# A hand-ordered two-stage Strassen MLP kernel: its order written anew, instruction by instruction

## The chip, the core and the metric

The kernel runs on one core of one Trainium2 chip. The metric is the device time of one execution in microseconds, as the median of several runs. TensorE (PE) does the matrix products, and its loading of weights is shown as a row of its own (PEld). VectorE (DVE), ScalarE (ACT) and GpSimd (POOL) do the elementwise work, and SyncE (SP) issues most of the loads and stores.

## The reference

```python
# x (8, 4096, 192); weight (8 heads, 7 taps); 24 channels to a head
w = softmax(weight, axis=-1)
x_pad = concat([zeros(8, 6, 192), x], axis=1)
out = einsum('hk,bskhg->bshg', w, x_pad[:, s + k, h, g])   # causal depthwise convolution
h = out.reshape(32768, 192) @ w_in                          # w_in (192, 2048)
g = h * (1 / (1 + exp(-1.702 * h)))
return g @ w_out                                            # w_out (2048, 192)
```

Everything is float32.

## The kernel before

The 32768 tokens are worked off in `N_BIG` = 32 steps of 1024 tokens. Both matrix products are done by schemes of the Strassen kind, which need fewer multiplications and more sums of operands and results. Steps 0 and 1 (`OPENING`) also prepare the weights; steps 2 to 31 all look alike. A step has two stages.

**First stage** (`product1`, L598). There are 20 products (`TERMS`) for each of two halves of the hidden width, and each of them is issued for two row halves, h = 0 and h = 1, on the two groups of 64 rows of the array: 80 matmuls of 64x128 weights on 512 columns. The trace shows a float32 matmul as two records, so these are 160 records. They go into four pairs of PSUM banks (`slot00`/`slot01` to `slot30`/`slot31`; the second digit is h), which are handed round through the list `free`; names such as a3 stand for a pair of banks, names such as k4 for a place in SBUF (`rooms`). Between the products, DVE forms sums (L639), ACT copies banks out (L633, or L635 into another bank) and applies the activation (L615 for one bank, L620 for a sum that covers two banks). A product into a bank waits until whoever reads the bank's last value is done.

**Second stage** (`second`, `one_matmul`, L855). 78 main parts of three matmuls each (column groups 0 to 2 of the array) and 78 side matmuls (column group 3), each 128x32 weights on 256 columns: 312 matmuls, 624 records. ACT copies results (L880, L884), DVE joins (L355, L357) and transposes them (L771), and SP stores.

**Beside the two stages**, work for later steps is spread over the same engines: DVE transposes x for the step after next into the tile `xt` (L438), ACT multiplies the taps (L483), POOL adds them up (L501) or issues adding DMAs (L506), POOL forms the sums of blocks that the products need (`vsum`, L355 and L357), and SP issues the DMAs that take a block to the other row half (`cross`, L526). DVE also forms the sums of the activated values g (`sum_g`, L355 and L357, 128x1024), part of them into `osbs`, and POOL issues adding DMAs for more of them (`acc`, L831).

What sets the order: each engine works through its instructions in the order in which the program issues them. For the first stage that is the list `ORDER`; there `do` issues both row halves of an entry one after the other. For the second stage it is `PLAN`, where an entry `go` issues one main part and then one side matmul. The spread work stands in queues (`todo`, `ready`, `adds`, `pieces`, `sums_left`) from which an entry such as `("tap",)` or `("vsum",)` takes the next piece, whatever it is.

Of the kernel before, what the change touches and what calls it, by code (L numbers as in the profile page):

```python
# [15 lines left out]
def kernel(  # L16
# [38 lines left out]
    xt_pool = ctx.enter_context(tc.tile_pool(name="xt", bufs=1))  # L55
# [6 lines left out]
    xts = {}  # L62
# [103 lines left out]
    def side(big, other, b):  # L166
        return cross_of(big, b) if other else slot_of(big, b)
# [20 lines left out]
    def form(i):  # L188
# [8 lines left out]
    COPY_O = [  # L197
        [(10, 2), (16, 1), (17, 0), (18, 0), (8, 7), (9, 5), (11, 3, -1), (12, 6, -1)],
        [(13, 3), (14, 3), (15, 0), (19, 4), (20, 4), (21, 5), (22, 7)],
        [],  # L200
        [(23, 1), (24, 1), (1, 14), (7, 0, -1)],
    ]
    SUMS_O = [
# [4 lines left out]
    ]  # L208
    TURN_O = (9, 17, 20, 21)

# [105 lines left out]
    def split_rest(i, part=slice(0, PIECE)):  # L316

        lo, hi, m, e = words(i, part)
        ef = e.bitcast(F32)
        act.activation(ef, e, AF.Relu, bias=bias[:, 0:1], scale=-1.0)  # L320
        act.activation(e, ef, AF.Relu, bias=bias[:, 1:2], scale=-(2.0**23))
# [43 lines left out]
    w_left = list(SUMS_W)  # L365

    def next_w(n):
        for _ in range(n):
            add_up(lambda j: w_in_s[:, j, :], *w_left.pop(0))

# [6 lines left out]
    def round_o(i):  # L377
# [15 lines left out]
        round_piece(NW + i, dsts)  # L393

    def add_forms(stage):
        for dst, src, *sign in COPY_O[stage]:
            if sign:
                act.mul(form(dst), form(src), -1.0)
            else:
                act.copy(form(dst), form(src))  # L400
        for dst, src in SUMS_O[stage]:
            nc.gpsimd.dma_start(out=form(dst), in_=form(src), accum_op=ALU.add)

    def end_forms():
        for i in TURN_O:
            act.mul(form(i), form(i), -1.0)
# [26 lines left out]

    def transpose_x(big, c, n=None):
        if big not in xts:
            xts[big] = xt_pool.tile([P, NC, 2, XT], F32, name="xt")
        ns = slice(0, 2) if n is None else slice(n, n + 1)
        vec.transpose(  # L438
            xts[big][:, c, ns, :].rearrange("p n (j t) -> p (n j) t", t=Q),
            xin[:, ns, :, :].rearrange("p n j d -> p (n j) d")[:, :, c * R : c * R + Q],  # L440
        )
# [10 lines left out]
    def tap_home(big, c, k):  # L452
        if big == 1:
            return homes_1[c][k - 1]
        if big < 3:
            return (first_taps if c == 0 else taps[3])[k - 1]
        return taps[c][k - 1]

    def conv_src(big, c, k, ns=slice(0, 2)):
        return xts[big][:, c, ns, Q - PAD + k : Q - PAD + k + T]  # L460

    def conv(big, c, k, ns=slice(0, 2), times=vec.tensor_scalar_mul):
        src = conv_src(big, c, k, ns)
        dst = own(big)[:, 2 * c + ns.start : 2 * c + ns.stop, :]
        tap = cw[:, c, k : k + 1]
        if k == 0:
            times(dst, src, tap)
# [5 lines left out]
    DMA_TAPS = (0,)  # L473
    TAPS_IN = (0, 2, 1)
    ADDS_IN = [(1, 6), (2, 5), (2, 6)] + [(c, k) for c in (2, 1) for k in range(1, K) if (c, k) not in ((1, 6), (2, 5), (2, 6))]
    TREE = {2: [(1, 2)], 4: [(3, 4)], 6: [(5, 6), (0, 1), (3, 5), (0, 3)]}
    TREE_1 = {2: {2: [(1, 2)], 4: [(3, 4), (0, 1)], 6: [(5, 6), (0, 3), (0, 5)]}, 0: {2: [(1, 2)], 4: [(3, 4)], 6: [(5, 6)]}}

    def tap(big, c, k):

        dst = own(big)[:, 2 * c : 2 * c + 2, :]
        home = tap_home(big, c, k) if k else dst
        act.mul(home, conv_src(big, c, k), cw[:, c, k : k + 1])  # L483
        if k and c not in DMA_TAPS and big > 1:
            adds.append((ADDS_IN.index((c, k)), dst, home))
            adds.sort(key=lambda a: a[0])
            if big == 2:
                next_add()
            return
        homes = [dst] + [tap_home(big, c, i) for i in range(1, K)]  # L490
        for a, b in (TREE if big > 1 else TREE_1[c]).get(k, ()):
            tree.append((homes[a], homes[b]))
        if big < 3:
            end_taps(2 if big == 2 and k == K - 1 else 0)

    tree, adds = [], []

    def next_add():
        if adds:
            _, dst, home = adds.pop(0)  # L500
            nc.gpsimd.tensor_add(dst, dst, home)  # L501

    def add_taps():
        if tree:
            out, src = tree.pop(0)
            nc.gpsimd.dma_start(out=out, in_=src, accum_op=ALU.add)  # L506

    def add_pair(c, a, b):

        dst = own(1)[:, 2 * c : 2 * c + 2, :]  # L510
        homes = [dst] + [tap_home(1, c, i) for i in range(1, K)]
        vec.tensor_add(homes[a], homes[a], homes[b])

    def end_taps(left=0):
        while len(tree) > left:
            add_taps()
# [13 lines left out]
    def copy_over(b):  # L530

        for o in range(2):
            act.copy(conv_t[halves[1 - o], cross_of(0, b), :], own(0)[halves[o], b, :])

    pieces, sums_left = [], []
    LAST_AT = {s[0]: i for i, s in enumerate(SUMS_C)}
    ENDS = (NBLK, NBLK + 3, NBLK + 6, NB - 2, NB)
    GROUPS = [range(*ends) for ends in zip(ENDS, ENDS[1:])]  # L540

    def cross_piece():
        if pieces:
            cross(*pieces.pop(0))

    def cross_blocks(big):

        bs = list(REST)
        while bs:
            n = 1  # L550
            while n < min(3, len(bs)) and bs[n] == bs[0] + n:
                n += 1
            pieces.append((big, bs[0], bs[0] + n))
            bs = bs[n:]

    def next_sum():
        if sums_left:
            big, i = sums_left.pop(0)
            sums_c(big, *SUMS_C[i])
            for b in GROUPS:  # L560
                if max(LAST_AT[s] for s in b) == i:
                    pieces.append((big, b[0], b[-1] + 1))

    def begin_sums(big):
        sums_left.extend((big, i) for i in range(len(SUMS_C)))

    def prepare(big):

        for k in range(K if big < 3 else 0):
            yield "", 0.76 if k else 0.48, lambda k=k: conv(big, 1, k)  # L570
        yield f"conv {big}", 0.0, lambda: None
        def done():
            need(f"taps {big}")
            while adds:
                next_add()
            if OPEN_SUM:
                sums_c(big, *OPEN_SUM)
            cross(big, OPEN, OPEN + 1)

        yield f"done {big}", 0.0, done  # L580

    def prepare_taps(big):

        order = [(c, k) for c in (0, 2) for k in range(K)]
        if big > 2:
            order = [(c, 0) for c in TAPS_IN] + [(c, k) for c in TAPS_IN for k in range(1, K)]
        for c, k in order:
            yield "", 1.0, lambda c=c, k=k: tap(big, c, k)
        yield f"taps {big}", 0.0, lambda: None

    def product1(slot, a, b, big, v, first=False):
# [3 lines left out]
        for h in range(2):  # L595
# [11 lines left out]
    ALL = slice(0, TOK)  # L607

    def gelu(b, u, v, src, sign=1):
# [3 lines left out]
        if isinstance(src, list):  # L613
            for h in range(2):
                act.activation(  # L615
                    dst[:, :, h, :], src[h].rearrange("p (o t) -> p o t", o=2), AF.Gelu_apprx_sigmoid,
                    scale=float(sign),
                )
        else:
            act.activation(  # L620
                dst.rearrange("p o h t -> p h o t"),
                src.rearrange("p h (o t) -> p h o t", o=2),
                AF.Gelu_apprx_sigmoid,
                scale=float(sign),
            )
# [3 lines left out]

    def copy2(dst, src, sign=1):  # L630
        for h in range(2):
            if sign == 1:
                act.copy(bank(dst, h), bank(src, h))  # L633
            else:
                act.mul(bank(dst, h), bank(src, h), -1.0)  # L635

    def sum2(op, dst, a, b):
        for h in range(2):
            op(*(bank(t, h) for t in (dst, a, b)))  # L639

# [623 lines left out]
```

## Time and profile before

| | before |
|---|---|
| median of 3 runs | 2262.73 us (2262.1 to 2263.56) |
| profiled execution | 2262.78 us, span 2261.1 us |
| busy PE / PEld | 2248.2 us (99%) / 1552.0 us (69%) |
| busy DVE / ACT / POOL | 1985.3 (88%) / 1707.7 (76%) / 1063.9 us (47%) |
| first stage of a steady step | 35.42 us |
| second stage of a steady step | 33.94 us |

A row of the chain or of the timeline begins with the start and the duration in microseconds; then come engine, tiles and line, and in brackets the idle time before it with what ended it. A group of instructions by line shows busy time and the mean of one in ns. PE counts as busy while a matmul is in flight on any part of the array, so a gap on one row group of the array does not show in PE's busy share; it shows in the length of a stage.

### The profile page before, as it was taken

To read this page: it belongs to the slowest core of one execution; us is meant where nothing else is said; L and a number is where in the kernel's file an instruction comes from. 1 tells how busy PE (TensorE), PEld (TensorE's weight loads), DVE (VectorE), ACT (ScalarE), POOL (GpSimd) and SP (SyncE) were. 2 spreads that over 40 slices of the span, in tenths; PEclk is the share of its full clock that TensorE was granted. 3 is DMA by queue.
4 is the path that set the end of the run, shared out by engine and by line. 5 is a ranking of instruction groups with operands and counts; after the bars stand their busy time and mean duration, and the time that the engine had idled before them with its cause. 6 is when DMAs were issued, how large, how long until landed. Compare 5 with 4: busy or idle time off the path is not lost.

```text
span 2261.1 us, 62136 instructions
## 1 busy us (share of the span) xinstructions
PE 2248.2 (99%) x24966; PEld 1552.0 (69%) x24966; DVE 1985.3 (88%) x2970; ACT 1707.7 (76%) x3233; POOL 1063.9 (47%) x1098
## 2 busy tenths in 40 slices
PE   9999999999999999999999999999999999999999
PEld 5366567766777766777667776667776677766775
DVE  8998888988889888889888898888988888988888
ACT  8677877777777778777787777787777877777754
POOL 1545544455543555444555445554355544455510
PEclk9999999999999999999999999999999999999999
DMA  8986657766667666576565776666866657765543
GB/s 198 174 158 133 125 114 150 143 128 127 121 131 159 128 128 126 111 160 140 125 132 114 141 152 128 129 124 118 163 134 128 124 114 151 144 127 103 104 92 71
DMA packets 275679, 298.05 MB, mean 132 GB/s; under 512 B 119104, under 2 KB 203328, under 8 KB 275392
## 3 DMA queue, kind: packets, MB, share of 16 engines
q0 software_dynamic: 57648, 150.69, 37.0%
q1 hardware_dynamic: 216096, 142.99, 27.8%
q8 instruction: 198, 3.24, 0.6%
q14 instruction: 89, 0.73, 0.1%
q10 hardware_dynamic: 1648, 0.39, 0.1%
HBM read 53.15 MB, written 25.17 MB: 35 GB/s over the span
## 4 chain that ended last, share of the span: by engine, by line
PE 96%; DVE 2%; ACT 1%; issue 1%; DMA 1%; POOL 0%; DVEq 0%; ACTq 0%; POOLq 0%; SPq 0%
PE slot L598 49%; PE slot L855 45%; PE slot L1120 1%; DVE g L357 1%; DMA g<-osbs 0%; PE slot L1115 0%; DVE room L357 0%; ACT g L615 0%; PE slot L946 0%; DVE room L639 0%; ACT w_form L483 0%; DMA xin<-in_x_dram 0%; DVE slot L639 0%; DVE room L355 0%; DVE osbs L771 0%
## 5 line engine op out<-in xcount | busy, mean ns | idle before, releaser
L598 PE MATMUL slot<-conv_t,w_in_s 64*128 64x512 f32 x5152 | 1147.4, 594 | 3.3 <-ACT room L633 1.5
L598 PEld LDWEIGHTS slot<-conv_t,w_in_s 64*128 64x128 f32 x5152 | 663.3, 186 | 474.6 <-issue 312.1
L855 PE MATMUL slot<-g,w_form 128*32 128x256 f32 x9672 | 894.2, 379 | 0.7 <-DVE room L357 0.7
L855 PEld LDWEIGHTS slot<-g,w_form 128*32 128x32 f32 x9672 | 575.6, 110 | 128.9 <-DVE room L357 2.1
L501 POOL TENSOR_TENSOR conv_t<-conv_t,g 128x512 f32<-128x512 f32 x354 | 449.0, 1275 | 88.4 <-ACT g L483 65.4
L855 PE MATMUL slot<-g,w_out_s 128*32 128x256 f32 x5952 | 467.5, 379 | 1.3 <-DVE g L357 0.8
L357 DVE TENSOR_TENSOR g<-g 128x1024 f32<-128x1024 f32 x372 | 450.4, 1224 | 8.0 <-DMA g<-osbs 1.0
L880 ACT COPY room<-slot 32x256 f32<-32x256 f32 x651 | 237.2, 364 | 289.8 <-PE slot L855 281.5
L639 DVE TENSOR_TENSOR room<-slot,room 128x512 f32<-128x512 f32 x620 | 383.6, 679 | 67.8 <-PE slot L598 67.8
L633 ACT COPY room<-slot 128x512 f32<-128x512 f32 x620 | 337.7, 595 | 77.7 <-PE slot L598 61.7
L483 ACT ACTIVATE g<-xt,cw 128x512 f32<-128x512 f32 x534 | 353.9, 715 | 3.7
L620 ACT ACTIVATE g<-room 128x1024 f32<-128x1024 f32 x248 | 265.7, 1071 | 79.0 <-DVE room L639 49.3
L615 ACT ACTIVATE g<-slot 128x512 f32<-128x512 f32 x528 | 282.5, 610 | 51.9 <-PE slot L598 32.8
L831 POOL DMA_DIRECT2D g<-g x124 | 128.1, 1038 | 355.0 <-PE slot L855 330.8
L639 DVE TENSOR_TENSOR slot<-slot,room 128x512 f32<-128x512 f32 x372 | 239.7, 689 | 53.8 <-PE slot L598 52.2
L855 PEld LDWEIGHTS slot<-g,w_out_s 128*32 128x32 f32 x5952 | 239.7, 110 | 43.2 <-DVE room L639 23.3
L355 POOL TENSOR_TENSOR conv_t<-conv_t 128x256 f32<-128x256 f32 x210 | 179.3, 860 | 129.2 <-PE slot L598 119.6
L855 PE MATMUL slot<-osbs,w_form 128*32 128x256 f32 x2232 | 229.5, 379 | 0.0
L506 POOL DMA_DIRECT2D g<-g x120 | 105.9, 883 | 238.1 <-ACT g L483 99.4
L855 PEld LDWEIGHTS slot<-osbs,w_form 128*32 128x32 f32 x2232 | 132.5, 110 | 23.6
L639 DVE TENSOR_TENSOR slot<-room,slot 128x512 f32<-128x512 f32 x124 | 79.8, 687 | 41.8 <-PE slot L598 41.8
L855 PE MATMUL slot<-room,w_form 128*32 128x256 f32 x1488 | 112.9, 379 | 0.0
(166 smaller groups left out, 1662.6 us busy)
## 6 DMA issues: line engine op xcount, KB each, us to landing
g<-g POOLq DMA_DIRECT2D x124, 512.0 KB, 6.5
xin<-in_x_dram SPq DMA_DIRECT2D x240, 180.0 KB, 4.2
conv_t<-conv_t SPq DMA_DIRECT2D x186, 192.0 KB, 5.4
g<-g POOLq DMA_DIRECT2D x120, 256.0 KB, 5.4
conv_t<-conv_t SPq DMA_DIRECT2D x186, 128.0 KB, 2.9
out_dram<-osbs SPq DMA_DIRECT2D x186, 128.0 KB, 2.7
g<-room POOLq DMA_DIRECT2D x31, 512.0 KB, 5.1
conv_t<-g POOLq DMA_DIRECT2D x60, 256.0 KB, 5.4
```

Source lines behind the costliest of these rows:

```text
L355: eng.tensor_add(v(dst), v(a), v(b))
L357: eng.tensor_sub(v(dst), v(a), v(b))
L483: act.mul(home, conv_src(big, c, k), cw[:, c, k : k + 1])
L501: nc.gpsimd.tensor_add(dst, dst, home)
L598: nc.tensor.matmul(slot[h], w_in_s[halves[h], a, v * P : (v + 1) * P], src, start=first, stop=True, skip_group_check=True,)
L615: act.activation(dst[:, :, h, :], src[h].rearrange("p (o t) -> p o t", o=2), AF.Gelu_apprx_sigmoid, scale=float(sign),)
L620: act.activation(dst.rearrange("p o h t -> p h o t"), src.rearrange("p h (o t) -> p h o t", o=2), AF.Gelu_apprx_sigmoid, scale=float(sign),)
L633: act.copy(bank(dst, h), bank(src, h))
L639: op(*(bank(t, h) for t in (dst, a, b)))
L831: nc.gpsimd.dma_start(out=spot(dst), in_=spot(a), accum_op=ALU.add)
L855: nc.tensor.matmul(dst, w, t, start=first, stop=last, skip_group_check=True)
L880: act.copy(to, d)
```

## The change

`ORDER`, `PLAN`, and the queues with their functions are replaced by one list, `STEP`, in which each entry issues one instruction (steps 2 to 30), and a list `LAST` for step 31. A product, a copy, a sum or an activation now names its row half h in its last place (None is the activation over both banks), so the two halves can stand apart; `("m", i)` is main part i, `("s", i)` side matmul i and `("t", i)` the copy of a side result. Taps, adds, block sums, crossings and x transposes are named one by one with the step they are for (a 1 or 2 ahead of the other numbers: the next step or the one after). `OPENING` is written out in the same way, in about the order of before. `xt` becomes a lasting tile, where before each step took a new one from a pool that holds one. The number of compute instructions on each engine stays.

```diff
-    xt_pool = ctx.enter_context(tc.tile_pool(name="xt", bufs=1))
+    xt = consts.tile([P, NC, 2, XT], F32)
...
-        if big not in xts:
-            xts[big] = xt_pool.tile([P, NC, 2, XT], F32, name="xt")
...
-    def product1(slot, a, b, big, v, first=False):
+    def product1(slot, a, b, big, v, first=False, hs=range(2)):
...
-        for h in range(2):
+        for h in hs:
...
-    def copy2(dst, src, sign=1):
-        for h in range(2):
...
-    ORDER = [
-        (0, "prod", 6, "a8"), (0, "sum", "k0", "a8", "-", "k8"), (0, "prod", 2, "a3"), (0, "copy", "k4", "a3", 1),
...
-    PLAN = [
-        ("side", 13, 16, "k0"), ("main", 1, 5, "p2", 1), ("vsum",), ("go", 2), ("sum", 14, 14, "-", 18), ("go", 1),
...
+    STEP = [
+        ("tap", 1, 1, 6), ("prod", 0, 6, "a8", 0), ("sum", 0, "k0", "a8", "-", "k8", 0), ("prod", 0, 2, "a3", 1),
...
+        ("prod", 1, 7, "a4", 0), ("gelu", 1, 1, 1, "a3", 1, 1), ("vsum", 1, 0), ("add", 1, 2, 4), ("vsum", 1, 1),
+        ("vsum", 1, 2), ("prod", 1, 15, "a3", 0), ("gelu", 1, 1, 1, "a3", 1, 0), ("prod", 1, 7, "a4", 1),
+        ("prod", 1, 1, "a1", 1), ("vsum", 1, 4), ("vsum", 1, 3), ("gsum", 0, 5, "+", 6), ("vsum", 1, 5),
+        ("prod", 1, 1, "a1", 0), ("sum", 1, "k3", "a4", "+", "k4", 0), ("sum", 1, "k3", "a4", "+", "k4", 1),
+        ("gelu", 1, 3, 1, "k3", 1, None), ("prod", 1, 10, "a4", 0), ("copy", 1, "a5", "a4", -1, 0),
...
-                w, t = now["steps"].pop(0)
-                for c in range(NC):
-                    one_matmul(chunk(now["to"], c), w[:, chunk_cols(c)], t, now["first"], not now["steps"])
-                now["first"] = False
-                d, ws, ts, st, to = side.pop(0)
-                one_matmul(d, ws, ts, st, to is not False)
+    def main_part(i):
+        dst, w, t, first, last = now["todo"][i]
+        for c in range(NC):
+            one_matmul(chunk(dst, c), w[:, chunk_cols(c)], t, first, last)
...
+    def side_part(i):
+        d, w, t, first, to = now["aside"][i]
+        one_matmul(d, w, t, first, to is not False)
```

Three places show how the instructions move. The first is ACT at the start of a steady step's first stage. `slot20`/`slot21` hold a3, `slot10`/`slot11` first a0 and then a4, `slot00`/`slot01` a1; L483 is a tap. Before:

```order
L633 COPY room_76<-slot20_71 128x512
L633 COPY room_76<-slot21_72 128x512
L483 ACTIVATE g_75<-xt_9955,cw_143 128x512
L633 COPY room_76<-slot10_69 128x512
L633 COPY room_76<-slot11_70 128x512
L633 COPY room_76<-slot00_67 128x512
L633 COPY room_76<-slot01_68 128x512
L615 ACTIVATE g_75<-slot20_71 128x2x256
L615 ACTIVATE g_75<-slot21_72 128x2x256
L620 ACTIVATE g_75<-room_76 128x2x2x256
L635 ACTIVATE slot20_71<-slot10_69 128x512
L635 ACTIVATE slot21_72<-slot11_70 128x512
```

The same place of the changed program, where L444 is the tap, L535 the copy out, L498 the activation and L537 the copy into another bank:

```order
L444 ACTIVATE g_72<-xt_142,cw_140 128x512 x3
L535 COPY room_73<-slot21_69 128x512
L535 COPY room_73<-slot10_66 128x512
L535 COPY room_73<-slot11_67 128x512
L535 COPY room_73<-slot20_68 128x512
L535 COPY room_73<-slot00_64 128x512
L535 COPY room_73<-slot01_65 128x512
L498 ACTIVATE g_72<-slot21_69 128x2x256
L498 ACTIVATE g_72<-slot20_68 128x2x256
L537 ACTIVATE slot20_68<-slot10_66 128x512
L537 ACTIVATE slot21_69<-slot11_67 128x512
```

The tap between the two pairs of copies has moved ahead of them, the copies take the half h = 1 of a3 first and its half h = 0 last, and the activation over two banks no longer stands ahead of the copies from `slot10` and `slot11` into another bank.

The second place is DVE in the second half of the first stage. The rows are the sums a4, k3, k5, a6 and a7 with the sums of g into `osbs` between them. Before:

```order
L639 TENSOR_TENSOR slot30_73<-slot10_69,room_76 128x512
L639 TENSOR_TENSOR slot31_74<-slot11_70,room_76 128x512
L639 TENSOR_TENSOR room_76<-slot30_73,room_76 128x512
L639 TENSOR_TENSOR room_76<-slot31_74,room_76 128x512
L639 TENSOR_TENSOR room_76<-slot20_71,room_76 128x512
L639 TENSOR_TENSOR room_76<-slot21_72,room_76 128x512
L355 TENSOR_TENSOR osbs_77<-g_75 128x1024
L357 TENSOR_TENSOR osbs_77<-g_75 128x1024
L639 TENSOR_TENSOR slot10_69<-room_76,slot30_73 128x512
L639 TENSOR_TENSOR slot11_70<-room_76,slot31_74 128x512
L357 TENSOR_TENSOR osbs_77<-osbs_77,g_75 128x1024
L639 TENSOR_TENSOR slot00_67<-slot30_73,room_76 128x512
```

Of the changed program (L343 and L341 are subtraction and addition):

```order
L343 TENSOR_TENSOR slot30_70<-slot10_66,room_73 128x512
L343 TENSOR_TENSOR slot31_71<-slot11_67,room_73 128x512
L341 TENSOR_TENSOR osbs_74<-g_72 128x1024
L341 TENSOR_TENSOR room_73<-slot30_70,room_73 128x512
L341 TENSOR_TENSOR room_73<-slot31_71,room_73 128x512
L343 TENSOR_TENSOR room_73<-slot20_68,room_73 128x512
L343 TENSOR_TENSOR room_73<-slot21_69,room_73 128x512
L343 TENSOR_TENSOR osbs_74<-g_72 128x1024
L343 TENSOR_TENSOR slot11_67<-room_73,slot31_71 128x512
L343 TENSOR_TENSOR slot10_66<-room_73,slot30_70 128x512
L343 TENSOR_TENSOR osbs_74<-osbs_74,g_72 128x1024
L341 TENSOR_TENSOR slot01_65<-slot31_71,room_73 128x512
```

The first sum into `osbs` has moved ahead of the sums k3, the second stays ahead of a6 and the third ahead of a7, and a6 and a7 begin with h = 1.

The third place is PE in the second stage. Rows with x3 are the three matmuls of a main part, the others are side matmuls. Before, close to the stage's start:

```order
L855 MATMUL slot00_67<-g_75,w_out_s_80 32x256 x3
L855 MATMUL slot01_68<-g_75,w_form_81 32x256
L855 MATMUL slot00_67<-g_75,w_form_81 32x256 x3
L855 MATMUL slot31_74<-g_75,w_form_81 32x256
L855 MATMUL slot00_67<-g_75,w_form_81 32x256 x3
```

The first rows of the stage in the changed program:

```order
L741 MATMUL slot11_67<-g_72,w_form_78 32x256 x2
L741 MATMUL slot00_64<-g_72,w_out_s_77 32x256 x6
L741 MATMUL slot01_65<-g_72,w_form_78 32x256 x2
L741 MATMUL slot00_64<-g_72,w_out_s_77 32x256 x3
L741 MATMUL slot00_64<-g_72,w_form_78 32x256 x3
L741 MATMUL slot00_64<-g_72,w_out_s_77 32x256 x3
L741 MATMUL slot31_71<-g_72,w_form_78 32x256 x2
L741 MATMUL slot00_64<-g_72,w_form_78 32x256 x3
L741 MATMUL slot11_67<-g_72,w_form_78 32x256
```

Where main parts and side matmuls took turns, two side matmuls now stand together, then two main parts, and so on.

More of the change, by code (lines that the diff above doesn't have):

```diff
@@ L1211 @@
[L1211 to L1233 removed]
+            fcopy=form_copy,
@@ L1237 @@
+    run(LAST, N_BIG - 1)
 _INS = ['x', 'weight', 'moe_w_in', 'moe_w_out']
```

754 lines of the change are left out of this document (296 added, 458 removed), and 381 rows, old and new, of tables (LAST, MAINS, OPENING, ORDER).

## The prediction

> **What bounds the kernel now.** I read the page first: the busy times, the granted clock, the chain that ended last.
>
> ```profile
> PE 2248.2 (99%) x24966; PEld 1552.0 (69%) x24966; DVE 1985.3 (88%) x2970; ACT 1707.7 (76%) x3233; POOL 1063.9 (47%) x1098
> PEclk9999999999999999999999999999999999999999
> PE 96%; DVE 2%; ACT 1%; issue 1%; DMA 1%; POOL 0%; DVEq 0%; ACTq 0%; POOLq 0%; SPq 0%
> L598 PE MATMUL slot<-conv_t,w_in_s 64*128 64x512 f32 x5152 | 1147.4, 594 | 3.3 <-ACT room L633 1.5
> ```
>
> TensorE is on 96% of the chain, its clock is granted in full throughout, and almost no idle time is listed ahead of its matmuls (3.3 us for L598). The loss hides in the lengths of the stages, because one row group counts as busy while the other waits. So next I read the chain in order of time: the end of step 1, the first stage of step 3, a late step, and the first stage of the last.
>
> ```profile
> 158.08 14.95 PE slot L855 x272
> ...
> 243.81 35.42 PE slot L598 x157
> ...
> 1978.56 35.42 PE slot L598 x157
> 2013.98 33.94 PE slot L855 x624
> ...
> 2186.62 35.07 PE slot L598 x153
> ```
>
> A steady step is 35.42 + 33.94 = 69.36 us. What would it be with nothing waited for? The timeline of weight loads shows a change from the second stage to the first, then, further on, a stretch without a stall; the third fence is a stretch of matmuls in the second stage.
>
> ```profile
> 1006.98 0.11 PEld L855 LDWEIGHTS slot<-g,w_form 128*32 128x32 f32 x1
> 1007.50 0.30 PEld L598 LDWEIGHTS slot<-conv_t,w_in_s 64*128 64x128 f32 x4 [0.41 <-issue]
> ```
>
> ```profile
> 1030.08 0.26 PEld L598 LDWEIGHTS slot<-conv_t,w_in_s 64*128 64x128 f32 x2 [0.17 <-issue]
> ...
> 1034.80 0.26 PEld L598 LDWEIGHTS slot<-conv_t,w_in_s 64*128 64x128 f32 x2 [0.17 <-DVE room L639]
> ```
>
> ```profile
> 1054.97 3.83 PE L855 MATMUL slot<-g,w_form 128*32 128x256 f32 x65
> ```
>
> In the first stage 11 rows of two loads lie between 1030.08 and 1034.80: 4.72 / 22 = 0.2146 us a record, so 160 records take 34.33. In the second stage 65 records are 16 sets of four and one more: (3.83 - 0.38) / 16 = 0.2156 a set, so 156 sets take 33.63. Together 67.96; a steady step loses 1.40 us. Not all of that can be won. From 1006.98 to 1007.50 the array changes its tiling: 0.52 where the pace is 0.215, a loss of 0.30, with nothing waited for. There are two such changes in a step, and the change of the program leaves both. What an order can win at most is 1.40 - 0.60 = 0.80 us a step.
>
> **Where the 0.80 goes.** The same timeline shows each place where loads come late.
>
> ```profile
> 1010.19 0.19 PEld L598 LDWEIGHTS slot<-conv_t,w_in_s 64*128 64x128 f32 x2 [0.24 <-issue]
> 1010.78 6.89 PEld L598 LDWEIGHTS slot<-conv_t,w_in_s 64*128 64x128 f32 x33 [0.40 <-ACT room L633]
> 1017.91 0.52 PEld L598 LDWEIGHTS slot<-conv_t,w_in_s 64*128 64x128 f32 x3 [0.24 <-issue]
> 1018.82 0.29 PEld L598 LDWEIGHTS slot<-conv_t,w_in_s 64*128 64x128 f32 x2 [0.39 <-POOL conv_t L501]
> ```
>
> ```profile
> 1036.12 0.29 PEld L598 LDWEIGHTS slot<-conv_t,w_in_s 64*128 64x128 f32 x2 [0.20 <-ACT slot L635]
> 1036.62 0.29 PEld L598 LDWEIGHTS slot<-conv_t,w_in_s 64*128 64x128 f32 x3 [0.21 <-ACT slot L635]
> ```
>
> ```profile
> 1041.87 0.29 PEld L598 LDWEIGHTS slot<-conv_t,w_in_s 64*128 64x128 f32 x2 [0.30 <-DVE slot L639]
> 1042.92 0.15 PEld L855 LDWEIGHTS slot<-g,w_out_s 128*32 128x32 f32 x6 [0.76 <-DVE room L639]
> ```
>
> Two loads should take 0.43. (1) 1010.19 to 1010.78 took 0.59, and the 33 records behind it 7.13 instead of 7.08: 0.21 lost on the copy k4 (L633). (2) The three records from 1017.91 took 0.91 instead of 0.64, and a part comes back in the records behind: about 0.15 net. (3) 1036.12 to 1036.62 took 0.50 on L635; with what comes back I count 0.14. (4) The rest, 0.80 - 0.50 = 0.30, is lost at the stage's end, where the last rows name DVE's sums.
>
> **What the change does to each.** The compute instructions stay the same in number on every engine, and both changes of tiling stay, so nothing is added or removed but waits. Each item is what the new order takes away.
>
> ```profile
> 1008.17 1.95 ACT L483 ACTIVATE g<-xt,cw 128x512 f32<-128x512 f32 x3
> 1010.14 1.07 ACT L633 COPY room<-slot 128x512 f32<-128x512 f32 x2
> ```
>
> ```profile
> 1016.85 1.06 ACT L620 ACTIVATE g<-room 128x1024 f32<-128x1024 f32 x1 [0.97 <-DVE room L639]
> 1018.17 1.07 ACT L635 ACTIVATE slot<-slot 128x512 f32<-128x512 f32 x2 [0.25 <-PE slot L598]
> ```
>
> (1) The copies k4 ran at 1010.14, behind three taps of 1.95 us in all, and product 14 overwrites what they read. From product 2 to product 14 there were 6 matmuls on each half; now there are 8 on h = 1 and 7 on h = 0, at 0.43 each. The copy of h = 0 comes last of the four, behind that of k1, whose product is the eighth: 0.43 + 0.59 for that one and two copies of 0.54 are 2.1 us, and from the eighth matmul to the fourteenth, product 14, are 6 x 0.43 = 2.6. All 0.21 should go. The tap that stood between the pairs (0.65) is moved ahead, where ACT had taps anyway. (2) ACT waited 0.97 for DVE to feed the activation over two banks (1.06), and L635 stood behind it; product 19 waits for L635. That activation now stands behind L635: the 0.15 goes. What is late next there is DVE's sum k5, one place later. (3) In the second half the same activation still stands ahead of the copy into another bank, but the products around it are spread: I count half, 0.07. (4) The end of the stage hangs on DVE, whose sums into `osbs` run beside POOL's block sums.
>
> ```profile
> L357 DVE TENSOR_TENSOR osbs<-osbs,g 128x1024 f32<-128x1024 f32 x31 | 52.2, 1685 | 0.0
> L355 DVE TENSOR_TENSOR osbs<-g 128x1024 f32<-128x1024 f32 x31 | 43.1, 1391 | 0.0
> L357 DVE TENSOR_TENSOR osbs<-g 128x1024 f32<-128x1024 f32 x31 | 37.7, 1216 | 0.0
> ```
>
> ```profile
> 1032.55 0.73 POOL L357 TENSOR_TENSOR conv_t<-conv_t 128x256 f32<-128x256 f32 x1
> ```
>
> ```profile
> 1039.60 1.60 POOL L355 TENSOR_TENSOR conv_t<-conv_t 128x256 f32<-128x256 f32 x1
> ```
>
> Three sums of one shape take 1.69, 1.39 and 1.22 on the mean of 31 steps, and a POOL sum 0.73 or 1.60: the two engines hold each other up, for 0.47 + 0.18 = 0.65 us of DVE a step. The third sum, the one of 1.69, stands right ahead of the last sums of the stage. In the new list `vsum` 4, 3, 5 lie around the first `osbs` sum and 7, 8 around the second, and by the third only a crossing is left: its 0.47 should be gone from the end. But the end hangs on PE's own last products and their sums too, as the last step shows, which has no block sums and is only 0.35 shorter (35.07); I count 0.08 of the 0.30.
>
> Sum: 0.21 + 0.15 + 0.07 + 0.08 = 0.51 us a step. Ends: 0.80 if every stall goes; below, -0.2 if the new waits outweigh (the 1.69 sum ahead of a tight one, less the gains). I take 0.5 for the 28 steps from 3 to 30: 14.0. Step 2 lasted from 158.08 + 14.95 = 173.03 to 243.81, 1.4 longer than a steady step, with waits on step 1's leftovers that a written list may spread; I count 0.5 of it. The last step: 0.3. The opening is in about its old order, and the tail is left at what lies behind 2186.62 + 35.07 and a second stage of 33.9, 5.5 us to the span's end: 0. Extra waits on SP delay no load that PE waits for by these rows: 0. The lasting `xt` lets a transpose start when its own readers are done, and no stall above names one: 0.
>
> The profiled execution took 2262.78 (span 2261.1 and 1.7 around it), 0.05 above the median of 2262.73. 2262.8 - 14.0 - 0.5 - 0.3 = 2248.0.
>
> **The rivals.** *TensorE keeps matmuls strictly in order (slower).* The new second stage has two side matmuls in a row, then two main parts. If a matmul cannot start ahead of one that waits for its own column group, the second of two neighbours holds up the other groups. Going through `STEP` by that rule, its 78 main parts and 78 side matmuls need 87 turns instead of 78 (`LAST` 86); a turn is 33.94 / 78 = 0.435. That is 9 x 0.435 = 3.9 us a step, 117 in all: 2248 + 117 = 2365. In the first stage neighbours of one row group are made good by the next matmul: 40 turns as before. It decides from one matmul that has to wait behind a neighbour of the same group.
>
> ```profile
> 1042.92 0.42 PE L855 MATMUL slot<-g,w_out_s 128*32 128x256 f32 x3
> 1043.11 0.38 PE L855 MATMUL slot<-g,w_form 128*32 128x256 f32 x1
> 1043.16 0.39 PE L855 MATMUL slot<-g,w_out_s 128*32 128x256 f32 x3
> ```
>
> Against it: the first records of three main matmuls start together, the side matmul's first at 1043.11, and the second records of the mains only at 1043.16. A side matmul thus started ahead of records that stand before it in the program. That is one record; the order before never had two neighbours of a group in the second stage, so it does not show whether three can be passed. The Trainium skill, "TensorE: Matmul & The Clock Gate", section "The mechanism", says that matmuls keep strict program order in start and end and only weight loads are pulled ahead. By that rule the time would be 2365; the three rows agree with it for whole matmuls and not for single records.
>
> *DVE and POOL collide at a tighter place (about as before).* The first `osbs` sum now stands between the sums a4 and k3, and product 10 overwrites what k3 reads. On its row group three products lie between (7, 15, 1): 3 x 0.858 = 2.57 us. In that time DVE has the second a4 (0.69), the `osbs` sum (1.22 to 1.69) and the first k3 (0.68): 2.59 to 3.06. If a4 is done only just in time, PE waits 0.02 to 0.49 at a place where it did not wait before; at 0.45 the gain is eaten: about 2262. The Trainium skill, "SBUF — State Buffer", section "Who interferes with whom", says that a DVE instruction with two SBUF inputs and a GpSimd one that reads SBUF exclude each other for a whole instruction. The rows agree (0.73 became 1.60); by that rule a wait could reach 0.73, which would make it 2267.
>
> *Every stall goes.* 0.80 x 29 + 1.4 = 24.6: 2238. For it: none of the rows above names an engine that is full. Against it: DVE is 88% busy.
>
> *The order moves the waits and not the sum.* If the stalls follow the chain from product to sum to product, they reappear one bank later: 2261.
>
> **How the numbers follow.** Forecast 0.48 (its own range 2241 to 2257), all stalls gone 0.14, collision 0.20 (2256 to 2268), strict order 0.12, waits only moved 0.06. A measurement of this kernel tells 0.2%, 4.5 us, from no change. Faster: 0.48 + 0.14 + 0.05 of the collision's = 0.67. Same: 0.06 + 0.08 = 0.14. Slower: 0.07 + 0.12 = 0.19. The range 2237 to 2268 holds all but the strict order and the edges.
>
> **What would show it.** Right: steady stages of about 34.9 and 33.9 in the chain; the gap ahead of the record at 3 us into the first stage back at 0.24, no wait on the copy into another bank at 11 us; one `osbs` sum of 1.22 at the end. Strict order: a second stage of 37.8. Collision: a wait on DVE some 23 us into the first stage. Wrong altogether: a first stage that is still 35.4, or a second stage that loses more than the first gains.

## The result, and the profile after

| | before | after |
|---|---|---|
| median | 2262.51 us (2262.1 to 2263.56, 4 runs) | 2239.9 us (2239.51 to 2240.3, 4 runs) |
| ratio | | 0.9899 (0.9882 to 0.9917) |
| span of the profiled execution | 2261.1 us | 2238.5 us |
| first stage of a steady step | 35.42 us | 34.80 us |
| second stage of a steady step | 33.94 us | 33.83 us |

The change is worth 22.6 us. The busy lines of the changed kernel's page would not tell this: PE's share stays at 99%, and VectorE, ScalarE and GpSimd are 7, 12.5 and 16 us busier.

```profile
PE 2226.1 (99%) x24966; PEld 1386.1 (62%) x24966; DVE 1992.3 (89%) x2970; ACT 1720.2 (77%) x3233; POOL 1079.6 (48%) x1098
PE 97%; DVE 1%; ACT 1%; issue 0%; DMA 0%; SPq 0%; DVEq 0%; ACTq 0%
```

The chain in order of time, with steps 2 and 3, a steady step and the last:

```profile
172.76 35.17 PE slot L481 x159
207.93 33.89 PE slot L741 x624
241.81 34.94 PE slot L481 x158
276.75 33.89 PE slot L741 x624
...
1409.71 34.80 PE slot L481 x160
1444.52 33.83 PE slot L741 x624
...
2164.84 34.25 PE slot L481 x155
2199.08 33.36 PE slot L741 x608
```

A steady step takes 68.63 us where it took 69.36; 0.67 of it is above the pace of 67.96. The 28 steps from 3 to 30 last from 241.81 to 2164.84 now and lasted from 243.81 to 2186.62: 1923.0 against 1942.8, a gain of 19.8. Step 2 gained 1.7 (243.81 - 173.03 = 70.8 before, 241.81 - 172.76 = 69.05 after), and what is left, about 1.1, lies ahead of step 2, in the last step and in the tail.

Where in the first stage? The timeline of matmuls gives rows that can be counted. Before, from the last record of a second stage on, and the last 43 records of the first stage (the second stage starts at 1042.92):

```profile
1007.20 0.38 PE L855 MATMUL slot<-g,w_form 128*32 128x256 f32 x1
1007.51 12.91 PE L598 MATMUL slot<-conv_t,w_in_s 64*128 64x512 f32 x57
```

```profile
1033.09 9.91 PE L598 MATMUL slot<-conv_t,w_in_s 64*128 64x512 f32 x43
```

After, the same two places:

```profile
997.73 13.69 PE L481 MATMUL slot<-conv_t,w_in_s 64*128 64x512 f32 x62
```

```profile
1022.96 9.65 PE L481 MATMUL slot<-conv_t,w_in_s 64*128 64x512 f32 x43
1032.54 0.40 PE L741 MATMUL slot<-g,w_form 128*32 128x256 f32 x1
```

A row runs to the end of its last matmul, so 0.59 comes off. Each of the two row groups has half of the records, one in 2 x 0.2146 = 0.4292 us. Before, the 57th record, the 29th of the earlier group, started after 12.32 where 28 x 0.4292 = 12.02: 0.30 was lost, and the other group was later still. Now the 62nd, the 31st of the later group, starts after 13.10 where 30 x 0.4292 = 12.88: 0.22 is lost. The last 43 records begin with the later group's 59th. From it to the second stage 1042.92 - 1033.09 = 9.83 went by, and 9.58 do now, where 22 x 0.4292 = 9.44: 0.39 was lost and 0.14 is. So the gain lies in both parts.

Following the later of the two row groups through the steady steps of both traces, the stage's loss against its pace splits like this:

| place in the first stage | loss before | loss after |
|---|---|---|
| start, after the change of tiling | 0.11 | 0.11 |
| (1) 2 to 6 us in: products 14 and 9, k4 and k1 | 0.32 | 0.03 |
| (2) 11 us in: product 19 of the first half | 0.26 | 0.08 |
| (3) 20 to 33 us in: second half; before, product 19 again | 0.13 | 0.16 |
| (4) the last product, and the start of the second stage | 0.26 | 0.09 |
| sum | 1.08 | 0.47 |

In the third row the place has changed. The 0.13 at product 19 is gone; 0.11 came up at product 14, 21 us in, and 0.05 at product 5, 31 us in. The weight loads there, in the changed kernel:

```profile
1018.46 0.40 PEld L481 LDWEIGHTS slot<-conv_t,w_in_s 64*128 64x128 f32 x4 [0.58 <-ACT room L535]
...
1028.91 0.29 PEld L481 LDWEIGHTS slot<-conv_t,w_in_s 64*128 64x128 f32 x3 [0.20 <-DVE slot L343]
```

Product 14 waits there for ACT's copies k4, product 5 for DVE's sum a6.

### The profile page after: what moved, and what is told of

Its sections match the earlier page's. It is cut to its first block, busy times and chain, and to the rows that moved or that the text cites. A ratio compares the mean times of both kernels' runs of the same rounds, so it can differ in the third digit from the quotient of the medians.

```text
span 2238.5 us, 61844 instructions
## 1 busy us (share of the span) xinstructions
PE 2226.1 (99%) x24966; PEld 1386.1 (62%) x24966; DVE 1992.3 (89%) x2970; ACT 1720.2 (77%) x3233; POOL 1079.6 (48%) x1098
## 4 chain that ended last, share of the span: by engine, by line
PE 97%; DVE 1%; ACT 1%; issue 0%; DMA 0%; SPq 0%; DVEq 0%; ACTq 0%
PE slot L481 49%; PE slot L741 48%; DVE g L343 0%; DVE room L343 0%; ACT g L498 0%; DMA xin<-in_x_dram 0%; ACT w_form L444 0%; ACT conv_t L1115 0%; DVE osbs L514 0%; DVE xt L405 0%; ACT w_form L537 0%; DVE conv_t L439 0%; DVE room L341 0%; ACT conv_t L444 0%; SPq L76 0%
## 5 line engine op out<-in xcount | busy, mean ns | idle before, releaser
L741 PE MATMUL slot<-g,w_form 128*32 128x256 f32 x9672 | 966.7, 379 | 0.4 <-DVE room L343 0.4
L481 PEld LDWEIGHTS slot<-conv_t,w_in_s 64*128 64x128 f32 x5152 | 621.0, 186 | 498.2 <-issue 292.9
L741 PEld LDWEIGHTS slot<-g,w_form 128*32 128x32 f32 x9672 | 549.8, 110 | 253.3 <-ACT g L498 22.7
L535 ACT COPY room<-slot 128x512 f32<-128x512 f32 (+1 forms) x806 | 409.8, 540 | 225.6 <-PE slot L741 133.6
L741 PE MATMUL slot<-g,w_out_s 128*32 128x256 f32 (+1 forms) x6048 | 529.8, 383 | 1.7 <-DVE g L343 0.8
L343 DVE TENSOR_TENSOR g<-g 128x1024 f32<-128x1024 f32 x372 | 442.2, 1222 | 2.3
L343 DVE TENSOR_TENSOR room<-slot,room 128x512 f32<-128x512 f32 x620 | 361.9, 626 | 13.8 <-PE slot L741 1.1
L444 ACT ACTIVATE g<-xt,cw 128x512 f32<-128x512 f32 x534 | 347.4, 712 | 5.9 <-DVE g L343 0.3
L498 ACT ACTIVATE g<-slot 128x512 f32<-128x512 f32 x528 | 294.2, 603 | 53.2 <-PE slot L481 44.1
L741 PE MATMUL slot<-osbs,w_form 128*32 128x256 f32 x2232 | 300.0, 379 | 0.0
L341 POOL TENSOR_TENSOR conv_t<-conv_t 128x256 f32<-128x256 f32 x210 | 205.6, 991 | 170.5 <-PE slot L481 86.9
L498 ACT ACTIVATE g<-room 128x1024 f32<-128x1024 f32 x248 | 264.8, 1068 | 18.7 <-DVE room L343 11.7
L343 DVE TENSOR_TENSOR slot<-slot,room 128x512 f32<-128x512 f32 x248 | 163.2, 693 | 9.0 <-PE slot L481 6.6
L341 DVE TENSOR_TENSOR slot<-slot,room 128x512 f32<-128x512 f32 (+1 forms) x155 | 93.9, 642 | 78.0 <-PE slot L481 37.8
L341 DVE TENSOR_TENSOR room<-slot,room 128x512 f32<-128x512 f32 (+1 forms) x248 | 137.1, 554 | 25.7 <-PE slot L481 12.3
```

The costliest lines, as they stand in the source:

```text
L341: eng.tensor_add(v(dst), v(a), v(b))
L343: eng.tensor_sub(v(dst), v(a), v(b))
L444: act.mul(tap_home(big, c, k), conv_src(big, c, k), cw[:, c, k : k + 1])
L481: nc.tensor.matmul(slot[h], w_in_s[halves[h], a, v * P : (v + 1) * P], src, start=first, stop=True, skip_group_check=True,)
L498: act.activation(dst, src, AF.Gelu_apprx_sigmoid, scale=float(sign))
L535: act.copy(dst, src)
```

## The experiments

Lengths of stages below are those of a steady step in the profiled execution. An experiment is compared with the kernel it was made from.

**Does the collision of DVE and POOL make the end late?** First the kernel before with three entries for block sums moved.

```diff
-  (1, "prod", 17, "a1"), ("vsum",), ..., ("vsum",), ..., (1, "prod", 11, "a1"), ("vsum",),
+  (1, "prod", 17, "a1"), ..., (1, "prod", 11, "a1"),
...
-  ("main", 1, 5, "p2", 1), ("vsum",), ("go", 2),
+  ("main", 1, 5, "p2", 1), ("vsum",), ("vsum",), ("vsum",), ("vsum",), ("go", 2),
```

> The kernel before with three of POOL's block sums moved from beside the third osbs sum to the start of the second stage. Theory (the end of the first stage is late because DVE and POOL hold each other up there): the osbs sum of 1.69 us falls to about 1.22, the first stage from 35.42 to about 35.0, the total by about 11 us to 2251. Rival (the end hangs on the order of the products and halves, not on that sum): the sum gets shorter, the first stage stays at 35.35 or more, the total within 2 us of 2262.5.

2264.4 us, ratio 1.0008 (0.9998 to 1.0017); the third sum took 1.69 as before. It tells nothing: in a steady step no other POOL instruction stands between the old place and the new, so POOL's order, and with it the time at which it does them, stayed. The next two move something that POOL cannot pass.

```diff
-  ("g", 2), (1, "prod", 10, "a4"),                        # the adding DMA (acc 8 0)
+  (1, "prod", 10, "a4"),
...
-  (1, "gelu", 3, 0, "k9", 1), ("cross",), ("done",),
+  (1, "gelu", 3, 0, "k9", 1), ("cross",), ("done",), ("g", 2),
```

> The kernel before with POOL's adding DMA (acc 8 0) moved from the first stage to the start of the second, as in the changed kernel. POOL then reaches its block sums earlier, beside the first and second osbs sums and not beside the third. Theory (the collision with the third sum makes the stage's end late): the third sum falls from 1.69 to about 1.22, the first stage to about 35.1, the total by 7 to 9 us to 2255. Rival (the collision only moves to the first two sums, which stand in the same run of DVE work): 35.4 and 2262.8.

2399.5 us, ratio 1.0606 (1.059 to 1.0622). Neither theory saw the price: the DMA is now late for the second stage, which grows to about 38 us, with PE waiting 2.9 us in one place for DVE's sums of g. The collision moved on to the second `osbs` sum (1.72 on the mean, the third 1.35). The reason is in POOL's timeline, around the start of the second stage at 1024.29, and, in the second fence, of the changed kernel, whose second stage starts at 1032.54:

```profile
1024.45 0.74 POOL L355 TENSOR_TENSOR conv_t<-conv_t 128x256 f32<-128x256 f32 x1 [3.65 <-PE slot L598]
1025.13 0.86 POOL L831 DMA_DIRECT2D g<-osbs  x1
```

```profile
1028.68 0.86 POOL L531 DMA_DIRECT2D g<-osbs  x1
```

In this experiment the DMA stands behind a block sum that waits 3.65 us for PE. In the changed kernel its entry stands in the second stage as well, but that block sum stands behind it, and POOL issues it 3.9 us before the stage starts.

```diff
-  ("prod", 1, 17, "a1", 0), ("vsum", 1, 7), ...           # changed kernel, first stage
+  ("prod", 1, 17, "a1", 0), ("vsum", 1, 6), ("vsum", 1, 7), ...
-  ("vsum", 1, 6), ("s", 63), ...                          # second stage
+  ("s", 63), ...
```

> The changed kernel with POOL's block sum 6 back in the first stage ahead of block sum 7, so that POOL's run there is 0.73 us longer and block sum 8 falls beside the third osbs sum. Theory (collision): that sum grows from 1.22 to 1.4 to 1.7, the first stage from 34.80 to about 35.0, the total by about 6 us to 2246. Rival: DVE has a pause ahead of these sums (1.0 us), so 34.8 to 34.9 and 2240 to 2242.

2248.6 us, ratio to before 0.9939 (0.9924 to 0.9954), 8.6 us above the changed kernel. The groups by line, first of the changed kernel, then of this one:

```profile
L343 DVE TENSOR_TENSOR osbs<-osbs,g 128x1024 f32<-128x1024 f32 x31 | 37.8, 1218 | 0.0
```

```profile
L343 DVE TENSOR_TENSOR osbs<-osbs,g 128x1024 f32<-128x1024 f32 x31 | 52.4, 1690 | 0.0
```

And the timelines of one step. The changed kernel, DVE and POOL:

```profile
1028.76 1.22 DVE L343 TENSOR_TENSOR osbs<-osbs,g 128x1024 f32<-128x1024 f32 x1
```

```profile
1028.01 0.73 POOL L341 TENSOR_TENSOR conv_t<-conv_t 128x256 f32<-128x256 f32 x1
```

With the block sum back:

```profile
1032.95 1.75 DVE L343 TENSOR_TENSOR osbs<-osbs,g 128x1024 f32<-128x1024 f32 x1
```

```profile
1032.89 0.73 POOL L341 TENSOR_TENSOR conv_t<-conv_t 128x256 f32<-128x256 f32 x1
```

POOL's sum ends at 1028.74, just before DVE's begins; one block sum more on POOL, and it begins 0.06 us ahead of DVE's, which takes 0.53 longer. The first stage grows by 0.25 to 35.05. This is shown: the third sum's stretching reaches PE, and in this step the changed order avoids it by 0.02 us. The Trainium skill, "SBUF — State Buffer", section "Who interferes with whom", says that the ports which the two share are locked for one of them at a time, and that the order of issue decides who is held up. The last two rows agree: POOL is ahead by 0.06, and DVE pays. The changed kernel with (acc 8 0) back ahead of block sum 7 was meant for the same:

```diff
-  ("prod", 1, 17, "a1", 0), ("vsum", 1, 7), ...
+  ("prod", 1, 17, "a1", 0), ("acc", 8, 0), ("vsum", 1, 7), ...
-  ("s", 2), ("acc", 8, 0), ("m", 0), ...
+  ("s", 2), ("m", 0), ...
```

> The changed kernel with POOL's adding DMA (acc 8 0) back in the first stage ahead of block sum 7, where it stood in the order before. Theory (collision of DVE and POOL at the end): block sums 7 and 8 start later and fall beside the third osbs sum, which grows from 1.22 to 1.5 or more; the first stage grows from 34.80 to about 35.1, the total by 8 to 10 us to 2249. Rival (order of products): 34.8 and 2240, whatever the sum takes.

2240.4 us, ratio to before 0.9901 (0.9886 to 0.9916). The third sum rose only to 1.26 on the mean, so the collision was not restored, and the time stayed; it neither speaks for nor against. Last, the third sum taken out of the way in the kernel before:

```diff
-  (1, "gelu", 0, 1, "a1", 1), ("g", 4), (2, "prod", 0, "a3"), ...
+  (1, "gelu", 0, 1, "a1", 1), (2, "prod", 0, "a3"), ...
-  (1, "sum", "k9", "a4", "-", "k0"), (1, "gelu", 0, 0, "a6", 1), ...
+  (1, "sum", "k9", "a4", "-", "k0"), ("g", 4), (1, "gelu", 0, 0, "a6", 1), ...
```

> The kernel before with the third osbs sum moved on DVE from ahead of the sums a7 to behind the last sums of the first stage. Theory (before the end of the stage DVE works without a pause through osbs, osbs, a6, osbs, a7, and PE's last product 13 waits for a7): with 1.69 us taken out of that run, product 13 no longer waits, the first stage falls from 35.42 to about 35.0, the total by about 11 us to 2251.5; the start of the second stage no longer waits long. Rival (the end waits for PE's own products and sums): 35.3 or more, total within 3 us of 2262.8.

2268.5 us, ratio 1.0026 (1.0015 to 1.0036). The sum took 1.22, but the first stage won only 0.10 (35.32) and the second lost 0.28 (34.22). In the old order DVE's 0.47 at the end was thus not what ended last by itself: without it, something 0.1 us earlier did.

**What ends last at the change of stage?** The function `begin` of the changed kernel also gives the side products their banks in another order, which the forecast passed over: the first side matmul goes into `slot11`, where before it went into `slot01`, which the sum k7 of h = 1 reads last. Undone in the changed kernel, and done alone in the kernel before:

```diff
-  mains, sides = (bs[0], bx[0], by[0]), (by[1], bx[1], bs[1])
+  mains, sides = (bs[0], bx[0], by[0]), (bx[1], bs[1], by[1])
```

> The changed kernel with the side products' banks in the old order again: the first side matmul of the second stage goes into slot01, which the last sum k7 of half h = 1 reads, where the changed kernel takes slot11. Theory (part of what was won at the end of the first stage is that the second stage no longer waits for that sum): the second stage starts later, the first stage grows from 34.80 to 35.0 or 35.1, the total by 6 to 9 us to 2247. Rival (collision of DVE and POOL and the order of products are all of it): 34.8 and 2240.

2257.5 us, ratio to before 0.9978 (0.9969 to 0.9987), 17.5 above the changed kernel, twice what was expected. Weight loads around the start of the second stage, in the changed kernel and then with the old banks:

```profile
1031.09 0.69 PEld L481 LDWEIGHTS slot<-conv_t,w_in_s 64*128 64x128 f32 x4 [0.17 <-issue]
1032.54 0.11 PEld L741 LDWEIGHTS slot<-g,w_form 128*32 128x32 f32 x1 [0.76 <-ACT g L498]
```

```profile
1038.02 0.69 PEld L481 LDWEIGHTS slot<-conv_t,w_in_s 64*128 64x128 f32 x4 [0.17 <-issue]
1039.69 0.14 PEld L741 LDWEIGHTS slot<-g,w_form 128*32 128x32 f32 x2 [0.98 <-ACT g L498]
...
1040.92 0.11 PEld L741 LDWEIGHTS slot<-g,w_form 128*32 128x32 f32 x1 [0.60 <-DVE room L343]
```

From the last four loads to the first of the second stage it takes 1.67 us instead of 1.45, and 1.2 us on no weight load starts for 0.60, until a sum that reads the next bank is done. The first of these waits is put down to ACT, but DVE's timeline with the old banks, where the four sums are k7 and then k9, shows what fits it:

```profile
1038.34 2.53 DVE L343 TENSOR_TENSOR room<-slot,room 128x512 f32<-128x512 f32 x4
```

At 0.6 to 0.7 for one sum, the second of the four (k7 of h = 1) ends at about 1039.6, an estimate from this row, and the load starts at 1039.69. First stage +0.25, second +0.33. So the theory's half was found, and a second wait that nobody had named.

```diff
-  mains, sides = (bs[0], bx[0], by[0]), (bx[1], bs[1], by[1])
+  mains, sides = (bs[0], bx[0], by[0]), (by[1], bx[1], bs[1])
```

> The kernel before with the side products' banks in the new order, and nothing else. Theory: the first main part still waits for the sum k7 of h = 0 and the first side no longer for that of h = 1, so the first stage falls from 35.42 to about 35.1, the total by 6 to 9 us to 2255. Rival (PE's last product 13 is late by itself there, behind the collision): 35.3 or more and 2260 or more.

2264.9 us, ratio 1.0010 (1.0000 to 1.0019): not faster. The second stage fell to 33.81, as in the changed kernel, but the first rose to 35.61: the second row group's first records now wait at the start for a side result that ACT copies out late.

```profile
1007.78 0.29 PEld L598 LDWEIGHTS slot<-conv_t,w_in_s 64*128 64x128 f32 x2 [0.41 <-issue]
1008.50 10.16 PEld L598 LDWEIGHTS slot<-conv_t,w_in_s 64*128 64x128 f32 x49 [0.42 <-ACT room L880]
```

The rise itself shows only at the end. By product 19 of the first half the later row group has lost 0.69, as in the kernel before; but DVE's third sum starts 31.6 us into the stage where it started 31.4, and the 0.2 comes with the last products, which wait for the sums behind it.

**What was the wait 11 us into the stage?** The forecast said the activation over two banks. Moved behind the copies in the kernel before, and ahead of them in the changed one:

```diff
-  ("turn", 1), (0, "gelu", 3, 1, "k3", 1), (0, "prod", 17, "a1"), (0, "copy", "a5", "a4", -1), (0, "copy", "k6", "a2", 1),
+  ("turn", 1), (0, "prod", 17, "a1"), (0, "copy", "a5", "a4", -1), (0, "copy", "k6", "a2", 1), (0, "gelu", 3, 1, "k3", 1),
```

> The kernel before with the two-bank activation of the first half moved behind the copies a5 and k6 on ACT. Theory (PE's loss of 0.2 us at about 11 us into the stage is this activation standing ahead of L635): the first stage falls to about 35.2, the total by 5 to 6 us to 2257. Rival (the wait is on the product that feeds the copy, or a wait further on takes up what is won): the first stage stays at 35.4, the total within 2 us of 2262.5.

2268.1 us, ratio 1.0024 (1.0014 to 1.0033); 35.60. The loss at 11 us stayed, and a new one of 0.2 came at the end of the stage, where DVE's third sum again starts 0.2 later.

```diff
-  ("sum", 0, "k7", "a7", "-", "k6", 0), ("gelu", 0, 3, 1, "k3", 1, None), ...
+  ("sum", 0, "k7", "a7", "-", "k6", 0), ...
-  ("prod", 0, 10, "a4", 0), ("copy", 0, "a5", "a4", -1, 0), ...
+  ("gelu", 0, 3, 1, "k3", 1, None), ("prod", 0, 10, "a4", 0), ("copy", 0, "a5", "a4", -1, 0), ...
```

> The changed kernel with the two-bank activation of the first half (k3) moved back ahead of the copy into another bank (a5), as it stood before. Theory (ACT's order there is worth 0.15 to 0.2 us a step): the first stage grows from 34.80 to about 35.0, the total by 5 us to 2245. Rival (the products are spread enough that the copies wait for PE anyway): 34.8 and 2240.

2239.8 us, ratio to before 0.9900 (0.9883 to 0.9916); 34.80. The activation's place is worth nothing. The other cause that the lists allow is the order of two products:

```diff
-  ("prod", 0, 10, "a4", 0), ("copy", 0, "a5", "a4", -1, 0), ("prod", 0, 18, "a2", 1), ("prod", 0, 10, "a4", 1),
-  ("copy", 0, "a5", "a4", -1, 1), ("prod", 0, 18, "a2", 0),
+  ("prod", 0, 18, "a2", 0), ("prod", 0, 18, "a2", 1), ("prod", 0, 10, "a4", 0), ("copy", 0, "a5", "a4", -1, 0),
+  ("prod", 0, 10, "a4", 1), ("copy", 0, "a5", "a4", -1, 1),
...                                                        # the same in the second half
```

> The changed kernel with product 18 back ahead of product 10 in both halves, so that one product and not two lies between product 10 and product 19 on each row group, as before. Theory (PE's losses at about 11.5 us and 29 us into the stage are product 19 waiting for the copy a5 of product 10's result): they come back with 0.2 and 0.1 us a step; the first stage grows from 34.80 to about 35.05, the total by 7 to 9 us to 2248. Rival (it was the activation, the taps or a DMA): 34.8 and 2240.

2268.2 us, ratio to before 1.0025 (1.0016 to 1.0035): 28 above the changed kernel, and behind even the old one. The first stage takes 35.74. The weight loads 11 us into it:

```profile
1020.45 0.29 PEld L481 LDWEIGHTS slot<-conv_t,w_in_s 64*128 64x128 f32 x2 [0.69 <-ACT slot L537]
1020.94 0.29 PEld L481 LDWEIGHTS slot<-conv_t,w_in_s 64*128 64x128 f32 x3 [0.20 <-ACT slot L537]
```

PE waits for the copies of product 10's result again, and loses 0.56 on the later row group at (2) where the changed kernel loses 0.08, and 0.5 at the same product of the second half. In effect the edit moves product 18 of h = 0 alone: on h = 1 it stands ahead of product 10 in the changed kernel too, and ACT's order is the same. ACT's copies into another bank, in the changed kernel and then here:

```profile
1007.57 0.58 ACT L537 ACTIVATE slot<-slot 128x512 f32<-128x512 f32 x1 [1.18 <-PE slot L481]
1008.38 0.58 ACT L537 ACTIVATE slot<-slot 128x512 f32<-128x512 f32 x1 [0.22 <-PE slot L481]
```

```profile
1019.82 1.07 ACT L537 ACTIVATE slot<-slot 128x512 f32<-128x512 f32 x2 [2.04 <-PE slot L481]
```

In the changed kernel h = 0 has product 10 one place earlier than h = 1, and the two copies come apart; here both results are ready together, and the second copy is half a microsecond late for PE. The place was right, and the first stage grew by 0.94 where 0.25 was expected. In the kernel before, the loss at (1) had put one row group 0.3 behind the other, so the two copies cost less there. By product 19 the later group has lost 0.67 here and 0.69 in the kernel before: with (2) undone, nearly all that was won at (1) and (2) together is lost again.

**Does PE keep its matmuls in order?** Runs of up to eight side matmuls and eight main parts, and turns one by one:

```diff
-  ("s", 0), ("s", 2), ("m", 0), ("m", 2), ("s", 4), ("s", 7), ("m", 1), ("m", 4), ("m", 3), ...
+  ("s", 0), ("s", 2), ("s", 4), ("s", 7), ("s", 8), ("s", 10), ("s", 3), ("s", 5), ("m", 0), ("m", 2), ...
```

> The changed kernel with the second stage's matmuls in runs of up to 8 side matmuls and up to 8 main parts, each kind in its order, and the other engines' work in its order behind what it needs. Going through the list by the rule of strict order gives 132 turns of 0.435 us in place of 78: a second stage of 57 us and a total near 2950. Theory (a matmul passes others that wait for another column group): with no limit on how many, 33.9 to 35 and 2240 to 2275; with a limit of a few matmuls, in between, and its place shows the limit.

2752.1 us, ratio 1.2164 (1.214 to 1.2189); a second stage of 50.9. Its first rows:

```profile
1070.98 2.99 PE L1118 MATMUL slot<-g,w_form 128*32 128x256 f32 x13
1073.61 0.42 PE L1118 MATMUL slot<-g,w_out_s 128*32 128x256 f32 x3
```

Eight side matmuls stand ahead of the first main part. It starts after 13 records, in the middle of the seventh side matmul, with the eighth still waiting: a matmul passed one whole matmul that waited for another column group, and did not pass two for 2.6 us. Whether the limit counts matmuls or records the run does not tell. Strict order would give 132 x 0.435 = 57; passing one waiting matmul gives 49 by the same count. The Trainium skill, "TensorE: Matmul & The Clock Gate", section "The mechanism", has matmuls start and end in strict program order. The rows differ from it by the one matmul that was passed.

```diff
-  ("s", 0), ("s", 2), ("m", 0), ("m", 2), ("s", 4), ("s", 7), ("m", 1), ("m", 4), ("m", 3), ...
+  ("s", 0), ("m", 0), ("s", 2), ("m", 2), ("s", 4), ("m", 1), ("s", 7), ("m", 4), ...
```

> The changed kernel with main parts and side matmuls of the second stage taking turns one by one, as before, the rest in its order. Theory (two neighbours of one column group cost nothing and win nothing): a second stage of 33.8 to 33.9 and a total of 2240 to 2242. Rival (the new order of the second stage is what shortened it from 33.94 to 33.83): 33.95 and 2243 or more.

2243.5 us, ratio to before 0.9916 (0.9902 to 0.9931), 3.6 above the changed kernel; 33.91 and 34.85. So the neighbours cost nothing, and their order wins a little: 0.08 in the second stage.

## Why the prediction was right, and where it was not

The direction and the range held. The likeliest case, 2248, was 8 us too careful, and 2239.9 lies outside its own 2241 to 2257; it comes closest to the rival in which every stall goes (2238). That it does so is in part luck: not every stall went, and the forecast had put too much of the loss beyond reach. By its own steps:

- *The floor, 67.96 and 0.60.* The pace held, the 0.60 did not. The forecast counted 0.30 for each change of tiling. Before, from the last record of a second stage to the first of the next stage it took 0.31 (1007.20 to 1007.51), and it does so in the changed kernel: 0.09 above the pace of 0.2156. With 0.11 behind it (the table's first row) and the 0.09 that is left at (4), the two changes take 0.29. So 1.1 us a step could be won and not 0.80. The changed kernel is 0.67 above the pace: 0.29 for the changes, 0.27 of waits at (1), (2) and (3), and 0.11 in the second stage.
- *The losses of before.* Counted on the later row group they were 0.32 and 0.26 at (1) and (2), not 0.21 and 0.15: the forecast took rows of loads in which both groups are mixed.
- *(1), 0.21.* 0.29 was won. No experiment undid the order of the copies k4 and k1 alone; that they are the cause stays argued.
- *(2), 0.15.* 0.18 was won, but the step failed in its cause. It named the activation; both experiments on it gave nothing or a loss. The forecast's own row of L635 spoke against it: ACT stood idle for 0.25 ahead of the copies, and what it waited for was PE. The runs show product 10's place instead: on h = 0 two products now lie between it and product 19, not one, so that ACT's two copies come apart.
- *(3), 0.07.* Nothing was won on the whole, 0.13 before and 0.16 after. The wait at product 19 did go, and undoing product 10's place brought 0.5 back there; but new waits came up at products 14 and 5, which the forecast had not named.
- *(4), 0.08.* This term was mis-sized: 0.17 was won at the end of the first stage. Two things hold it together, the third sum free of the collision (0.25 when undone) and the new banks of the side products (0.25 there when undone). The forecast read the first and discounted it, and did not see the second. In the old order the new banks won nothing at this place: there a main part stood first, and not a side matmul.
- *The second stage, 0.* It won 0.11. Before, the first side matmul started 0.19 behind the main parts; now the two start together. The new banks alone bring the old kernel's stage to 33.81; in the changed kernel undoing them costs 0.33, undoing the neighbours 0.08.
- *Step 2, 0.5, and the last step, 0.3.* 1.7 and 0.8 were won, the 0.8 all in the last first stage (35.07 before, 34.25 now). No run took this apart.
- *The rivals.* Strict order fell, and narrowly: the new list needs one passed matmul, and one is what PE allows. The collision at a tighter place fell too: the first `osbs` sum, now ahead of k3, takes 1.22 on the mean, and the later row group loses nothing at product 10 of the second half, the place that this rival named. That the order only moves the waits came true at (3), and not on the whole. In the changed kernel's timelines of DVE and of POOL it is POOL that pays there, having started 0.22 us later:

```profile
1021.35 1.21 DVE L341 TENSOR_TENSOR osbs<-g 128x1024 f32<-128x1024 f32 x1
```

```profile
1021.57 1.58 POOL L341 TENSOR_TENSOR conv_t<-conv_t 128x256 f32<-128x256 f32 x1 [2.53 <-PE slot L481]
```

The undone parts add up to more than the whole (28.3 + 17.5 + 8.6 + 3.6 = 58.0, against a gain of 22.6 us), and every part done alone in the old order, as far as tried, won nothing or lost. The gain belongs to the list as a whole: each part is worth what the others leave it.

## What to carry to other kernels

When PE shows 99% busy, compare the length of a stage with its records times the pace, and follow the later row group: a wait on one group hides in the busy share. An experiment that moves an instruction in the program only moves it in time if something on its own engine stands between. Parts of a balanced order cannot be priced one at a time: read the slack of the place that comes last, and expect undoing a part to cost more than it won.

## What had not been expected

- In the second stage a matmul starts ahead of one that waits for another column group, and not ahead of two: eight side matmuls in a row held the main part back for 2.63 us.
- A block sum of POOL that starts 0.06 us ahead of DVE's sum of 128x1024 stretches it from 1.22 to 1.75 us; one that ends 0.02 us ahead does nothing.
- Which bank a side product takes moved 17.5 us of 2240, with no instruction more or less.
